# Hash-masked attention followed by an FNet mixing block: input tests and norm squares moved to the end of the kernel, and batch 0's work shared out anew between VectorE, ScalarE and TensorE

## The chip, the cores and the metric

The kernel runs on one core of a Trainium2 chip. A core has five engines that work at the same time, each through its own instructions in order: TensorE (PE, matrix products; its weight loads appear apart as PEld), VectorE (DVE), ScalarE (ACT), GpSimd (POOL) and SyncE (SP, which here only issues transfers). Transfers are issued by SP, ACT or POOL and carried by 16 DMA engines. The metric is the device time of one execution in microseconds (us), as the median of repeated runs; less is better. Beside it a profiler has recorded one execution instruction by instruction; that record is the trace.

## What is computed

```python
# attention, for q, k, v of shape (4, 8, 768, 64) and proj (64, 6)
q_bits = (np.einsum('bhsd,dk->bhsk', q, proj) > 0)
k_bits = (np.einsum('bhsd,dk->bhsk', k, proj) > 0)
mask   = q_bucket[:, :, :, None] == k_bucket[:, :, None, :]     # buckets: the 6 bits as a number
scores = np.where(mask, scale * q @ k.T, -1e9)
attn   = softmax(scores)            # max subtracted, sum + 1e-9
x      = (attn @ v)                 # heads side by side: (4, 768, 512)

# mixing block, w_ch1 (512, 2048), w_ch2 (2048, 512)
mixed = np.real(fft(fft(x, axis=1), axis=2))
u     = x + mixed
un    = (u - mean(u)) / sqrt(var(u) + 1e-6)
out   = u + np.maximum(un @ w_ch1, 0.0) @ w_ch2
```

The two weight matrices arrive as 64-bit floats, everything else as 32-bit floats.

## The kernel before, in words

**Work and stages.** The unit of attention is a pair of heads `n` (0 to 15, four to a batch). For each pair, `prepare(n)` turns q and k over so that the 64 features lie on the partitions and finds the hash bits; then six chunks `c` of 128 keys follow. For each chunk `weigh` (line 871) has TensorE make the scores in two halves of 384 queries for both heads, ScalarE takes the exponential of each half (line 897), and, one step later, `values` (909) has TensorE multiply the weights with v into two PSUM accumulators `oo` (914). The softmax needs the sum of the weights over all keys: VectorE adds the chunks up in `acc` (988), and at the end of a pair `scale` (919) lets TensorE sum `acc` over the partitions with a matrix of ones (932, four products of 32 columns each side by side), and the result divides `x`. When a batch is attended, `mix(b)` does the Fourier transforms (lines 1086 and 1115), the transposition (1141), and the two weight products `inner` (1390) and `outer7` (1270), both as a seven-product scheme over half-size blocks. In the time that `mix(b)` is at work, attention of batch b+1 runs interleaved with it; `mix(3)` runs alone at the end.

**How the mask is made.** For the pairs in `LITE` (0 to 4) the hash bits of q and k are written as small numbers into a tile `qkb`, and four extra 16-bit products per chunk (885) add a large negative number to scores whose buckets differ. `prepare` builds this tile with VectorE: one comparison for q (805), two products with the columns of a constant `own` (811, so that each head sees its own rows only), one comparison for k (805) and four copies of 32 partitions each (817). For the other pairs VectorE multiplies the exponentials with the mask (903).

**Inputs of 64 bits.** `weights1` fetches the first weight matrix in 16 slices of 512 KB into seven slots and `narrow` (628) makes 32-bit floats of each: VectorE takes the upper word apart (639, 643), ScalarE scales the lower word (647), VectorE adds (649). The slot is fetched into again once it has been read. `narrow` also tests that no number is too small for the short cut: ScalarE takes the absolute value of the upper word (654) and sums `Relu(least - |hi|)` into a column of `strange` (655, followed by a short read of the accumulator). `weights2` does the same for the second matrix during `mix(0)`, from POOL's queue with two slots. The kernel also guards against scores so large that the exponential without a subtracted maximum would be unsafe: `norm` (748) lets ScalarE sum the squares of q and of k for each pair into `norms` (750), within `prepare`. At the start of `mix(3)`, lines 1523 to 1539 reduce `norms` and `strange` to a single flag `fl` that all engines read; if it is set, a slower general kernel runs after this one. With the inputs of the reference the flag is 0.

**What sets the order.** Batch 0 lies within `manual_schedule` (1481): PE, DVE, ACT and POOL run exactly in the order in which the program text emits. There the generator `attention(0)` is advanced step by step (pair and chunk), and after four of five steps one step of `weights1` follows. After batch 0 a scheduler orders the instructions of each engine by its own estimate of when each can run; the text gives priorities. On each queue, an instruction that waits holds up all behind it.

**Buffers that matter here.** PSUM has two score tiles (tag `sc`), two accumulators (`o`) and two further banks (`ps`) for everything else, until `mix(3)` sets `roomy` and uses all six for its products. The exponentials go to two tiles `pk`. q and k of a pair share a tag `qkn` with two buffers, so that the next pair's q can be fetched only when this pair's q has been read by both the transposition (768) and the square (750). The folded input `z` of a batch is one buffer.

Of the kernel before, what the change touches and what calls it, by code (L numbers as in the profile page):

```python
# [485 lines left out]
def _main(  # L486
# [134 lines left out]


    least = const.tile([P, 1], F32, tag="least", name="least")
    nc.gpsimd.memset(least, float(897 << 20))
    strange = const.tile([P, 2 * NDC * DFF // WC], F32, tag="strange", name="strange")
    nc.gpsimd.memset(strange, 0.0)

    def narrow(dst, raw, col, low=None):


        lo, hi = (raw[..., i] for i in range(2))
        t = lo.bitcast(F32)
        if low is None:

            low, t = lo, hi.bitcast(F32)
        di = dst.bitcast(I32)


        nc.vector.tensor_scalar(
            di, hi, 3, (1 << 30) - 1,  # L640
            op0=ALU.logical_shift_left, op1=ALU.bitwise_and,
        )
        nc.vector.scalar_tensor_tensor(
            di, hi, -(1 << 30), di, op0=ALU.bitwise_and, op1=ALU.bitwise_or
        )

        nc.scalar.activation(low, lo.bitcast(U32), AF.Copy, scale=2.0**-29)
        if len(di.shape) == 2:
            nc.vector.tensor_tensor(di, di, low, op=ALU.add)
        else:  # L650
            for i in range(di.shape[1]):
                nc.vector.tensor_tensor(di[:, i], di[:, i], low[:, i], op=ALU.add)

        nc.scalar.activation(t, hi, AF.Abs)
# [25 lines left out]
    class Arrival:  # L680
# [30 lines left out]
    def weights1():  # L711
        slices = [
            (w1[:, c, f : f + WC], moe_w_ch1[c * P : (c + 1) * P, f : f + WC])
            for f in range(0, DFF, WC)
            for c in range(NDC)
        ]
        zt = wt([P, 3, 2 * WC], F32, "z", "zraw1", 1)
# [26 lines left out]
    xs = {}  # L744

    preps = {}

    def norm(n, io, tn):
        junk = wt([P, S], BF16, "junk", f"sq{io}_{n}", 1)
# [5 lines left out]
    def prepare(n):  # L755
# [3 lines left out]
        for io, nm in enumerate("qk"):  # L759
            tn = nat.pop((nm, n))  # L760
            tt = wt([P, S], F32, nm + "t", f"{nm}t{n}")
            if n > 0:
                to, at = tt, tn
                if nm == "q":

                    to = tt.rearrange("p (i r n) -> p r i n", i=2, r=2)
                    at = tn.rearrange("p (r i n) -> p r i n", i=2, r=2)
                nc.vector.transpose(to, at)
            for g in range(2) if n == 0 else ():
                ps = pt([P, 3, P], f"tr{nm}{n}_{g}")  # L770
# [15 lines left out]
            ts[nm] = tt  # L786
            yield
            norm(n, io, tn)
        if lite:


# [5 lines left out]
            for io, nm in enumerate("qk"):  # L797
                ps = pt([P, HALF], f"bits{nm}{n}")
                for j in range(4):
                    h, g = divmod(j, 2)  # L800
                    nc.tensor.matmul(
                        ps[32 * j : 32 * j + 32, :], pjw[:, h * D : h * D + 32],
                        ts[nm][:, g * HALF : (g + 1) * HALF], start=True, stop=True,
                    )
                nc.vector.tensor_scalar(
                    bits[nm], ps, 0.0, off[:, io : io + 1],
                    op0=ALU.is_gt, op1=ALU.subtract,
                )
                if io == 0:
                    for g in (1, 0):  # L810
                        nc.vector.tensor_scalar(
                            qz[:, g], qz[:, 0], own[:, g : g + 1], None, op0=ALU.mult
                        )
                else:
                    for j in range(4):
                        to, at = (slice(32 * i, 32 * i + 32) for i in (j, j ^ 1))
                        nc.vector.tensor_copy(qk[to, 1, HALF:S], qk[at, 1, 0:HALF])
                yield
            preps[n] = ts["q"], ts["k"], qk, None
            return  # L820
# [95 lines left out]
                    pk[:, g, h, 0:w], start=(c == 0), stop=(c == NT - 1),  # L916
                )

    def scale(n, oos, sums):


        x = xs[n // NPAIR][:, n % NPAIR]
# [6 lines left out]
        ps = pt([P, HALF], f"sum{n}")  # L929
        for i, part in enumerate(sums):  # L930
            for j in range(4):
                nc.tensor.matmul(
                    ps[32 * j : 32 * j + 32, :], ones, part[:, j // 2, j % 2],
                    start=(i == 0), stop=(i == len(sums) - 1),
                )


        rt = wt([P, S], F32, "rt", f"rt{n}", 1)
        nc.vector.transpose(rt[:, 0:HALF], ps)
# [14 lines left out]

    def attention(b):
        xs[b] = wt([P, NPAIR, S], F32, "x", f"x{b}")
        pending, scales = [], []

        def finish():
            n, c, pk, oos, sums = pending.pop(0)  # L960
            with behind() if n >= NPAIR and t is not None else nullcontext():
                values(n, c, pk, oos)
            if c == NT - 1:
                scales.append(scale(n, oos, sums))
                next(scales[-1])

        for t in range(NPAIR):
# [8 lines left out]
            for c in range(NT):  # L976
# [523 lines left out]
    for b in range(B):  # L1500
# [17 lines left out]
        if b == B - 1:  # L1518
            roomy[0] = True

            ms = const.tile([P, 3], F32, tag="ms", name="ms")
            nc.vector.tensor_reduce(ms[:, 0:2], norms, axis=AX.X, op=ALU.max)
            nc.vector.tensor_reduce(ms[:, 2:3], strange, axis=AX.X, op=ALU.max)
            ps = pt([1, 3, P], "norms_t")
            for io in range(3):
                nc.tensor.transpose(ps[:, io, :], ms[:, io : io + 1], ident)
            mt = const.tile([1, 5], F32, tag="mt", name="mt")
            nc.vector.tensor_reduce(mt[:, 0:3], ps, axis=AX.X, op=ALU.max)  # L1530
            nc.vector.tensor_tensor(mt[:, 3:4], mt[:, 0:1], mt[:, 1:2], op=ALU.mult)
            nc.vector.tensor_scalar(
                mt[:, 4:5], mt[:, 3:4], (SAFE / SCALE / 2) ** 2, None, op0=ALU.is_gt
            )
            fl = const.tile([1, 1], I32, tag="fl", name="fl")
            nc.vector.scalar_tensor_tensor(
                fl, mt[:, 2:3], 0.0, mt[:, 4:5], op0=ALU.is_gt, op1=ALU.max
            )
            large = nc.values_load(fl[0:1, 0:1], min_val=0, max_val=1)
# [54 lines left out]
```

## Time and profile before

| what | value |
|---|---|
| median of three runs | 1102.72 us (1101.38 to 1104.4) |
| the profiled execution, its own time | 1102.7 us |
| its span, from first to last instruction | 1100.4 us |
| TensorE busy in the span | 1043.3 us |
| VectorE busy | 790.5 us |
| ScalarE busy | 499.5 us |
| GpSimd busy | 58.6 us |
| batch 0's last product with v begins at | 112.17 us |
| `mix(3)` begins (first product of line 1086) at | 925.03 us |

How to read it: the span is 2.3 us shorter than the time that is reported for the same execution. A busy share is an average over stages with different limits, so the stages are looked at one by one: batch 0 up to about 114 us, the passage to batch 1 up to about 140 us, batches 1 to 3 with a mix beside them up to 925 us, and the last mix to the end. A timeline line gives the start, the duration, the engine, the line of the program, the operation with its output and input, how many were joined in one line, and in brackets how long the engine was idle before and what released it.

### The profile page before, as it was taken

What the parts mean: (1) busy time and instruction counts of PE and PEld (TensorE: products, weight loads), DVE (VectorE), ACT (ScalarE), POOL (GpSimd) and SP (SyncE); (2) the same over time, 40 slices, a digit from 0 to 9 for tenths busy, and PEclk for the clock granted to TensorE, in tenths of its full rate; (3) what the DMA queues carried; (4) which work ended last, traced back from release to release, by engine and by line L of the source; (5) the groups of instructions that cost most, each with busy time, mean ns of one, the idle gap of its engine ahead of it and who ended that gap; (6) DMA issues with size and microseconds to landing.
All of it is one profiled execution on the core that took longest, in us unless ns stands there. A gap on an engine that the chain in (4) does not pass through costs nothing.

```text
span 1100.4 us, 14144 instructions
## 1 busy us (share of the span) xinstructions
PE 1043.3 (95%) x4933; PEld 632.7 (57%) x4933; DVE 790.5 (72%) x1336; ACT 499.5 (45%) x1055; POOL 58.6 (5%) x132
## 2 busy tenths in 40 slices
PE   7989897999989999999999999999999999999996
PEld 3333353446744675545664576645674569768575
DVE  5899958878599977776767785965856785644353
ACT  6987555553276324454326433355315522340420
POOL 0000000002000020010000011001000002100000
PEclk9999999999999999999999999999999999999998
DMA  9755353451056161322154134213032205122301
GB/s 222 224 95 126 64 140 72 138 164 19 20 149 209 44 204 26 68 63 66 26 157 107 48 82 153 44 43 92 15 129 68 68 24 172 55 81 88 123 20 41
DMA packets 175710, 103.13 MB, mean 94 GB/s; under 512 B 129552, under 2 KB 162960, under 8 KB 175632
## 3 DMA queue, kind: packets, MB, share of 16 engines
q1 hardware_dynamic: 169840, 88.65, 30.1%
q0 software_dynamic: 4224, 13.11, 3.7%
q8 instruction: 41, 0.67, 0.2%
q10 hardware_dynamic: 1568, 0.39, 0.2%
q14 instruction: 37, 0.30, 0.1%
HBM read 81.14 MB, written 20.97 MB: 93 GB/s over the span
## 4 chain that ended last, share of the span: by engine, by line
PE 61%; DVE 11%; ACT 4%; DMA 2%; issue 2%; DVEq 0%; SPq 0%; ACTq 0%
PE o L1270 22%; PE h_p L1390 20%; PE oo L914 6%; PE sc L893 6%; DVE pk L903 3%; PE cs L1086 2%; DMA zraw<-in_moe_w_ch_dram 2%; PE A L1115 2%; PE B L1115 1%; DVE acc L988 1%; ACT rr L948 1%; DVE w L1282 1%; DVE h L1256 1%; PE bits L825 1%; PE un L1141 1%
## 5 line engine op out<-in xcount | busy, mean ns | idle before, releaser
L1270 PE MATMUL o<-w,h 128*128 128x256 f32 x1152 | 259.4, 382 | 1.2 <-ACT tq L1289 0.7
L1270 PEld LDWEIGHTS o<-w,h 128*128 128x128 f32 x1152 | 216.3, 190 | 43.6 <-issue 4.6
L897 ACT ACTIVATE pk<-sc 128x768 f32<-128x768 f32 x192 | 147.6, 809 | 78.4 <-PE sc L893 60.9
L1390 PE MATMUL h_p<-x,w 128*128 128x384 f32 x448 | 163.5, 495 | 3.2 <-ACT h L1412 1.5
L893 PE MATMUL sc<-qt,kt 64*128 64x384 f32 x768 | 155.7, 508 | 6.0 <-ACT pk L897 5.7
L914 PE MATMUL oo<-pk,vn 128*64 128x385 f32 (+1 forms) x768 | 155.3, 499 | 6.0 <-DVE pk L903 3.0
L903 DVE SCALAR_TENSOR_TENSOR pk<-qb,kb,pk 128x768 f32<-128x768 bf16 x132 | 129.0, 1012 | 30.2 <-ACT pk L897 30.1
L1390 PEld LDWEIGHTS h_p<-x,w 128*128 128x128 f32 x448 | 82.3, 190 | 71.0 <-ACT pk L897 5.4
L988 DVE TENSOR_TENSOR acc<-acc,pk 128x1536 f32<-128x1536 f32 (+1 forms) x72 | 105.7, 1482 | 7.2 <-ACT pk L897 6.7
L1390 PE MATMUL h_p<-w 128*128 128x384 f32 x288 | 105.5, 489 | 2.3 <-ACT w L1427 2.3
L914 PEld LDWEIGHTS oo<-pk,vn 128*64 128x64 f32 x768 | 49.1, 136 | 100.0 <-issue 69.3
L893 PEld LDWEIGHTS sc<-qt,kt 64*128 64x128 f32 x768 | 66.9, 188 | 51.3 <-issue 24.0
L1390 PEld LDWEIGHTS h_p<-w 128*128 128x128 f32 x288 | 53.7, 190 | 41.7 <-ACT w L1427 3.5
L1300 ACT COPY tq<-o 128x256 f32<-128x256 f32 x24 | 8.9, 372 | 105.1 <-PE o L1270 105.1
L1282 DVE SCALAR_TENSOR_TENSOR w<-o,rs,w 128x256 f32<-128x256 f32 x56 | 26.7, 478 | 41.6 <-PE o L1270 41.6
L1270 PE MATMUL o<-w 128*128 128x256 f32 x176 | 42.3, 383 | 1.3 <-DVE w L1282 1.3
L1416 DVE TENSOR_TENSOR h<-h 128x384 f32<-128x384 f32 x32 | 17.8, 556 | 33.1 <-ACT h L1415 33.1
L1289 ACT COPY tq<-o 128x256 f32<-128x256 f32 x24 | 8.9, 371 | 69.3 <-PE o L1270 69.2
L1270 PEld LDWEIGHTS o<-w 128*128 128x128 f32 x176 | 32.8, 190 | 8.8 <-DVE w L1282 2.9
L1423 DVE TENSOR_TENSOR h<-h 128x384 f32<-128x384 f32 x32 | 17.7, 553 | 27.0 <-ACT h L1422 27.0
L1024 POOL DMA_DIRECT2D out_dram<-w x30 | 16.4, 548 | 388.7 <-issue 293.2
L1086 PE MATMUL cs<-ch,z 128*128 128x128 f32 (+3 forms) x192 | 33.2, 324 | 3.0 <-DVE bt L829 1.9
(170 smaller groups left out, 1312.4 us busy)
## 6 DMA issues: line engine op xcount, KB each, us to landing
w<-ad SPq DMA_DIRECT2D x168, 128.0 KB, 2.0
w<-bd SPq DMA_DIRECT2D x42, 512.0 KB, 4.5
zraw<-in_moe_w_ch_dram POOLq DMA_DIRECT2D x16, 512.0 KB, 4.0
bd<-w SPq DMA_DIRECT2D x14, 512.0 KB, 3.9
vn<-in_v_dram SPq DMA_DIRECT2D x32, 192.0 KB, 3.4
qn<-in_q_dram SPq DMA_DIRECT2D x120, 48.0 KB, 2.4
kn<-in_k_dram SPq DMA_DIRECT2D x60, 96.0 KB, 3.4
zraw<-in_moe_w_ch_dram SPq DMA_DIRECT2D x8, 512.0 KB, 5.7
```

The source lines that it names most:

```text
L893: last[0] = nc.tensor.matmul(ps[:, h, 0:HALF], kt[rows, ks], qt[rows, qs], start=kb is not None, stop=True,)
L897: nc.scalar.activation(pk[:, g, :, 0:HALF], ps[:, :, 0:HALF], AF.Exp, scale=SCALE)
L903: nc.vector.scalar_tensor_tensor(w, qb[:, h].rearrange("p (g s) -> p g s", g=2), kb[:, h, c : c + 1], w, op0=ALU.is_equal, op1=ALU.mult,)
L914: nc.tensor.matmul(oos[g][h * D : (h + 1) * D, 0:w], nat["v", n][:, (2 * c + h) * D : (2 * c + h + 1) * D], pk[:, g, h, 0:w], start=(c == ...
L988: nc.vector.tensor_tensor(acc[:, g], (first if c == 1 else acc)[:, g], new[:, g], op=ALU.add,)
L1086: nc.tensor.matmul(ps[:, pc + 2 * lo : pc + 2 * hi - 1 : 2], z[:, cp, pc, par, t * P : (t + 1) * P], ch[:, cp, pc, lo:hi], start=(cp == 0) ...
L1115: nc.tensor.matmul(ps[:, cols], F[:, par, k, t, j * P : (j + 1) * P], sq[:, t, k, cols], start=(t == 0), stop=(t == 1),)
L1270: nc.tensor.matmul(ps, a[:, r], right7[i][:, r], start=start and r == 0, stop=r == HF // 2 - 1, skip_group_check=not start,)
L1282: nc.vector.scalar_tensor_tensor(t[:, cols], src, r, t[:, cols], op0=ALU.mult, op1=ALU.add)
L1390: nc.tensor.matmul(ps, left[:, k], right[i][:, k], start=start and k == 0, stop=k == 1, skip_group_check=not start,)
L1416: nc.vector.tensor_tensor(c21, c12, c21, op=ALU.add)
L1423: nc.vector.tensor_tensor(c22, c21, c22, op=ALU.add)
```

## The change

- In `weights1` the tests are no longer made (`col` is None). `narrow` makes them only where it is given a column, so `weights2` keeps its own; the test is now a function `in_range`, and compares the bits as floats.
- `prepare` makes the squares only for pairs from `LATER` = 8 on. The squares of pairs 0 to 7 and the tests of the first weight matrix go to a new generator `guard`, which fetches q and k of these pairs (16 loads of 384 KB) and the 16 slices of 512 KB a second time, all from POOL's queue, squares and tests them on ScalarE, and then makes the flag. It is advanced within the loop over `mix(3)`; the flag is read eight steps before the end of that loop. This part lies outside `manual_schedule`.
- For the pairs in `LITE`, ScalarE instead of VectorE makes the two products with `own` and the four copies.
- In batch 0 the weights of the fifth chunk are not added to `acc` by VectorE. TensorE sums them over the partitions in a product of their own with the matrix of ones, one step ahead of the pair's other sums and into the same PSUM bank `sum`, which is therefore taken a step earlier.

The order of the built program shows where the scheduler puts the work of `guard`: the 16 loads of q and k stand in POOL's queue after the last `rs` of `mix(2)`'s first half and ahead of all of its stores, and the 16 squares stand in ScalarE's queue between the first copy of line 1289 of `mix(2)`'s `outer7` (first half, j = 0) and the one of j = 2, among the exponentials of pair 14. Of the 16 tests, six stand after the last copy into `F` (1099) of `mix(3)` and ahead of the copies of line 1142, the other ten among the copies and activations of the first three steps of `inner`. The product `norms_t` stands in the first step of the second half of `inner`.

```diff
@@ weights1, narrow, test
-                narrow(dst, raw, self.col + i, low)
+                narrow(dst, raw, self.col and self.col + i, low)
...
-        arrival = Arrival(slices, raws, 0, nc.sync)
+        arrival = Arrival(slices, raws, None, nc.sync)
...
+        if col is not None:
+            in_range(raw, col, t)
+    def in_range(raw, col, t=None):
+        lo, hi = (raw[..., i].bitcast(F32) for i in range(2))
+        t = lo if t is None else t
         nc.scalar.activation(t, hi, AF.Abs)
         nc.scalar.activation(
             t, t, AF.Relu, bias=least, scale=-1.0, accum_out=strange[:, col : col + 1]
         )
@@ the late part
+    LATER = 2 * NPAIR
+    def guard():
+        for n in range(LATER):
+            b, t = divmod(n, NPAIR)
+            for io, src in enumerate((q, k)):
+                tn = wt([P, S], F32, "qkn", f"nn{io}_{n}", 2)
+                nc.gpsimd.dma_start(
+                    tn,
+                    src[b, 2 * t : 2 * t + 2].rearrange("h (p c) d -> (h p) (c d)", p=P // 2),
+                )
+                norm(n, io, tn)
+                yield
+        if wide:
+            raws = wt([P, 3, 2 * WC], F32, "z", "zlast", 1)
+            for i, (dst, src) in enumerate(slices1()):
+                raw = raws[:, i % 3].bitcast(I32)
+                nc.gpsimd.dma_start(raw.bitcast(I64), src)
+                in_range(raw.rearrange("p (n w) -> p n w", w=2), i)
+                yield
...
+        yield fl
@@ prepare
-            norm(n, io, tn)
+            if n >= LATER:
+                norm(n, io, tn)
...
-                        nc.vector.tensor_scalar(
-                            qz[:, g], qz[:, 0], own[:, g : g + 1], None, op0=ALU.mult
+                        nc.scalar.activation(
+                            qz[:, g], qz[:, 0], AF.Copy, scale=own[:, g : g + 1]
                         )
...
-                        nc.vector.tensor_copy(qk[to, 1, HALF:S], qk[at, 1, 0:HALF])
+                        nc.scalar.copy(qk[to, 1, HALF:S], qk[at, 1, 0:HALF])
@@ attention
+            if b == 0 and c == NT - 2:
+                total.append(pt([P, HALF], f"sum{n}"))
+                weight_sums(total[0], sums[:1], True, False)
             if c == NT - 1:
-                scales.append(scale(n, oos, sums))
+                scales.append(scale(n, oos, sums, total.pop() if total else None))
...
+                elif c == NT - 2 and b == 0:
+                    sums = [new]
@@ the end of the program
-            (reduction of norms and strange to fl, large = nc.values_load(fl ...))
...
-    for _ in other:
-        pass
+    checks = guard()
+    flag = None
+    for i, _ in enumerate(other):
+        if (i < 9 or i % 4 < 3) and flag is None:
+            flag = next(checks)
+        if i == MIX - 8:
+            large = nc.values_load(flag[0:1, 0:1], min_val=0, max_val=1)
```

More of the change, by code (lines that the diff above doesn't have):

```diff
@@ L623, in _main @@
     least = const.tile([P, 1], F32, tag="least", name="least")
-    nc.gpsimd.memset(least, float(897 << 20))
+    nc.gpsimd.memset(least, float(np.array(897 << 20, np.int32).view(np.float32)))
     strange = const.tile([P, 2 * NDC * DFF // WC], F32, tag="strange", name="strange")
@@ L652, in narrow @@
                 nc.vector.tensor_tensor(di[:, i], di[:, i], low[:, i], op=ALU.add)
+        if col is not None:
+            in_range(raw, col, t)
+    wide = moe_w_ch1.dtype == I64
+    def in_range(raw, col, t=None):
+        lo, hi = (raw[..., i].bitcast(F32) for i in range(2))
+        t = lo if t is None else t
         nc.scalar.activation(t, hi, AF.Abs)
@@ L707, in convert, with slices1 @@
                     raw = raw.rearrange("p (s n w) -> p s n w", w=2, n=dst.shape[-1])
-                narrow(dst, raw, self.col + i, low)
+                narrow(dst, raw, self.col and self.col + i, low)
             self.fetch(i + self.depth)
-    def weights1():
-        slices = [
+    def slices1():
+        return [
             (w1[:, c, f : f + WC], moe_w_ch1[c * P : (c + 1) * P, f : f + WC])
@@ L716, in weights1 @@
         ]
+    def weights1():
+        slices = slices1()
         zt = wt([P, 3, 2 * WC], F32, "z", "zraw1", 1)
@@ L746, in _main @@
     preps = {}
+    LATER = 2 * NPAIR
[17 more added lines that the diff above has]
+                yield
+        ms = const.tile([P, 3], F32, tag="ms", name="ms")
+        nc.vector.tensor_reduce(ms[:, 0:2], norms, axis=AX.X, op=ALU.max)
+        nc.vector.tensor_reduce(ms[:, 2:3], strange, axis=AX.X, op=ALU.max)
+        ps = pt([1, 3, P], "norms_t")
+        for io in range(3):
+            nc.tensor.transpose(ps[:, io, :], ms[:, io : io + 1], ident)
+        mt = const.tile([1, 5], F32, tag="mt", name="mt")
+        nc.vector.tensor_reduce(mt[:, 0:3], ps, axis=AX.X, op=ALU.max)
+        nc.vector.tensor_tensor(mt[:, 3:4], mt[:, 0:1], mt[:, 1:2], op=ALU.mult)
+        nc.vector.tensor_scalar(
+            mt[:, 4:5], mt[:, 3:4], (SAFE / SCALE / 2) ** 2, None, op0=ALU.is_gt
+        )
+        fl = const.tile([1, 1], I32, tag="fl", name="fl")
+        nc.vector.scalar_tensor_tensor(
+            fl, mt[:, 2:3], 0.0, mt[:, 4:5], op0=ALU.is_gt, op1=ALU.max
+        )
+        yield fl
     def norm(n, io, tn):
@@ L917, in values, with weight_sums, scale @@
                 )
-    def scale(n, oos, sums):
+    def weight_sums(ps, sums, first, last):
+        for i, part in enumerate(sums):
+            for j in range(4):
+                nc.tensor.matmul(
+                    ps[32 * j : 32 * j + 32, :], ones, part[:, j // 2, j % 2],
+                    start=first and i == 0, stop=last and i == len(sums) - 1,
+                )
+    def scale(n, oos, sums, ps=None):
         x = xs[n // NPAIR][:, n % NPAIR]
@@ L927, in scale @@
             nc.scalar.activation(xg, oos[g][:, 0:HALF], AF.Identity, bias=vs)
[L929 to L935, printed above, removed]
+        fresh = ps is None
+        if fresh:
+            ps = pt([P, HALF], f"sum{n}")
+        weight_sums(ps, sums, fresh, True)
         rt = wt([P, S], F32, "rt", f"rt{n}", 1)
@@ L956, in attention @@
         xs[b] = wt([P, NPAIR, S], F32, "x", f"x{b}")
-        pending, scales = [], []
+        pending, scales, total = [], [], []
         def finish():
@@ L1519, in _main @@
             roomy[0] = True
[L1523 to L1539, printed above, removed]
         for _ in other:
```

## The prediction

> **What bounds the kernel now.** I read the page first (busy shares, then the 40 slices), then the busy time of stretches, then ScalarE's timeline where the change inserts work. The page's busy part:
>
> ```profile
> PE 1043.3 (95%) x4933; PEld 632.7 (57%) x4933; DVE 790.5 (72%) x1336; ACT 499.5 (45%) x1055; POOL 58.6 (5%) x132
> ...
> DVE  5899958878599977776767785965856785644353
> ACT  6987555553276324454326433355315522340420
> ```
>
> TensorE bounds the whole; in the first slices (27.5 us each) VectorE and ScalarE are as full as it is, and ScalarE is nearly empty from slice 30 on. Batch 0 cut at the pairs' first scores, and the passage to batch 1 (start:end, length, then the busy time of PE, PEld, DVE, ACT):
>
> ```profile
> 12.00:34.80 22.80, 20.66 (x136) 8.60 (x136) 19.08 (x33) 19.08 (x32) 0.00 (x0) 1.00 0.98 304
> 34.80:63.35 28.55, 25.30 (x169) 9.70 (x167) 25.04 (x43) 24.43 (x50) 0.00 (x0) 1.00 0.60 135
> 63.35:87.77 24.42, 22.12 (x154) 8.84 (x155) 23.13 (x37) 23.93 (x50) 0.00 (x0) 1.00 0.57 96
> 87.77:113.70 25.93, 23.87 (x164) 8.99 (x166) 24.95 (x47) 18.52 (x38) 0.11 (x1) 1.00 0.51 120
> 113.70:139.70 26.00, 20.83 (x135) 8.96 (x133) 23.96 (x46) 13.98 (x32) 0.00 (x0) 1.00 0.41 80
> ```
>
> TensorE's idle time is 2.14, 3.25, 2.30, 2.06 and 5.17 us: 14.9 us, and no more than this can be won here, however much the other two engines lose. Where the late work goes (ScalarE's timeline, with idle time and releaser in brackets):
>
> ```profile
> 772.84 0.37 ACT L1289 COPY tq<-o 128x256 f32<-128x256 f32 x1 [2.02 <-PE o L1270]
> ...
> 785.87 0.37 ACT L1303 COPY tq<-o 128x256 f32<-128x256 f32 x1
> ...
> 811.14 0.37 ACT L1289 COPY tq<-o 128x256 f32<-128x256 f32 x1 [4.81 <-PE o L1270]
> ...
> 932.64 0.41 ACT L1099 COPY F<-cs 128x255 f32<-128x255 f32 x1
> 944.40 0.59 ACT L1142 COPY w<-un 128x512 f32<-128x512 f32 x1 [11.35 <-PE un L1141]
> ```
>
> ScalarE is idle here most of the time, but each of these copies empties a PSUM bank that TensorE wants next, and in both stretches TensorE has no idle time to give (35.45 of 36 us busy in 775 to 811, 28.00 of 28 in 945 to 973). What a load from POOL's queue takes:
>
> ```profile
> zraw<-in_moe_w_ch_dram POOLq DMA_DIRECT2D x16, 512.0 KB, 4.0
> ```
>
> **What the Trainium skill says.** "ScalarE: Activation LUTs", section "What ACT_TABLE_LOAD costs", gives an ACTIVATE 186 ns plus 0.833 ns an element, 93 ns more for a pointer operand, 93 ns of overlap back to back. The trace agrees: a copy of 384 took 0.48 us (506 ns by the page). "DMA: Bandwidth & Descriptors", section "Anatomy of one DMA — SWDGE (gpsimd) path", fits 2.0 us plus bytes/436e3; the 4.0 us above is longer than its 3.2, so I use only the slope. "TensorEngine Tiling (Array Packing)", section "Key Properties", has tiles work in parallel: four 32-column products of line 932 last 0.85 us together in the trace, though each lasts 0.5. "Advanced Engine Details and Errata", section "Sequencer and Instruction Queues", has instructions read in turn and each wait for its semaphores; the trace shows the consequence at 110.48, where a square idles ScalarE for 4.91 us on a load of k while ready exponentials stand behind it.
>
> **The change, part by part, against the profiled 1102.7 us.**
>
> *Removed in batch 0.* ScalarE: 16 tests of 0.685 + 0.78 + 0.19 (655's accumulator read) = 26.5 us, ten squares of 0.845 + 0.19 = 10.4. VectorE: ten products of 0.32, twenty copies of 0.25, eight additions of 0.95 = 15.8 us. *Added.* ScalarE: ten products (0.51 by the page named) and twenty copies (0.41): 13.3 us, the copies due only before the next pair's second score tile, so under cover; without it, 2.5 us a pair. TensorE: four times 0.7 us (the two sets of line 932 start 0.67 and 0.76 us apart) = 2.8 us, fully on the path.
>
> *Where the idle time goes, pair by pair.* Pair 0: gaps of 0.48, 0.36, 0.83 and 0.38 wait for exponentials behind tests; they go, 2.05. Less the sum, 1.35. Pair 1: VectorE runs without a pause from the pair's sum at 39.53 to the comparison at 58.07 for which TensorE waits; nothing in that row is removed, so the pair only inherits 1.35, then pays 0.7: 0.65. Pair 2: the gap of 1.93 at 76.27 (exponentials behind a test) shrinks to some 0.2, and 0.37 behind the products with `own` goes: 2.8, less 0.7, 2.1. Pair 3: the square named above waits no more, 2.06, less 0.7: 3.4. Passage: VectorE (23.96 of 26 busy) is the bound and has lost 3.6 us ahead of the sum's transposition (0.68 + 1.82 + 1.06), of which ScalarE's and TensorE's own order lets 1.6 through: **5.0 us won** at 140 us. From below 2 (the passage gives nothing and one gap stays), from above 10 (all but 2 of the 14.9 filled, less the 2.8 paid).
>
> *Squares of pairs 5 to 7* leave ScalarE in batch 1, 6 us of its time; TensorE waits for exponentials there twice (2.09 and 2.66 us). **0.5 us won**; between 2 won and 2 lost, since the scheduler reorders some copies there.
>
> *The 16 late squares.* A load of 384 KB lands after 4.0 less 131 KB at the page's slope, 3.7 us (estimate). Two buffers: q and k alternate, and each next load waits for the square before last. One pair of squares therefore takes 3.7 + 1.04 = 4.75 us, not 2.1. The first k can be fetched when k of pair 15 has been transposed (777.6); its square ends at 782.3, the eighth at 782.3 + 7 x 4.75 = 815.6. Behind it in ScalarE's queue stands the copy that now runs at 811.14: 4.5 us late. It starts earlier: the copy of 785.87 now stands behind the third k square, 791.8, and TensorE, with two banks, wants the next one at 788. Exponentials of pair 14 are held likewise. No slack follows in which TensorE could catch up: **4.5 us lost**. From below 1 (landing in 2.4 us, as the 48 KB pieces of q: last square at 805), from above 12 (5.55 us, the longest load of line 693 that the chain shows, with part of the 17 us covered by other products). POOL's stores stand behind these loads but come due only at 888.
>
> *The 16 late tests.* `zlast` is the buffer of `z`, read until 932.05, so the first slice lands at 936. Six tests of 1.65 us with three slots: three end at 941, the slots come back at 941.7, the sixth ends at 946.7; the copies of 944.40 are 2.3 late. The other ten, 16.5 us, meet 15.0 us of ScalarE work in the 28 us from 945 to 973: 3.5 over. The built order has one product moved ahead, 0.7 of cover: **5.1 us lost**. From below 2 (only the first six show), from above 10 (2.3, and each of the ten puts one of its 0.8 us halves in front of a copy that TensorE awaits). The load traffic, 14.7 MB, meets little: these stretches move 12, 1 and 92 GB/s.
>
> *The flag* moves from 900 to about 1028 us. `norms_t` costs TensorE 0.5 us in either place. On SP the read of the flag stands ahead of the last nine loads of the ring; the first is wanted by a product at about 1043, 12 loads ahead: nothing, unless the flag came 12 us late.
>
> Sum: 1102.7 - 5.0 - 0.5 + 4.5 + 5.1 = **1106.8 us**. The profiled run's own time and the median agree (1102.7 and 1102.72).
>
> **Rivals.** *Faster, 1097 us:* the late work is truly idle time's, and batch 0 gives twice my sum. For it: ScalarE is busy 10.6 of 36 us where the squares go. 1102.7 - 9 + 3.3. It decides from where loads land in under 2.7 us (a pair of squares in 3.7, last one at 807, ahead of its successor) and the passage gives 4 us. Against it: 4.0 us measured. *No difference, 1102.5:* the gain of 5.5 stands and half of each loss is covered by TensorE's reordered products; for it, the scheduler did move scores behind products in that stretch. *Much slower, 1115:* loads take 5 us and more, ScalarE stands before the squares and all exponentials with it. Against it, DMA is nearly idle. *That the change doesn't do what it says:* `weights2` keeps its 16 tests, so batch 1 gains nothing from them; counted.
>
> **From these to the numbers.** A difference under 0.3% (3.3 us: 1099.4 to 1106.0) can hardly be told from none. Chances: my forecast 0.52 (own range 1104.5 to 1110; 0.08 of it falls within 0.3%), much slower 0.14, no difference 0.17, faster 0.17. So faster 0.17, same 0.25, slower 0.58. The range 1098 to 1114 leaves out the ends of the first and the last rival.
>
> **What would show it.** Batch 0: last product with v at about 108 to 109 us instead of 112.17, no square before a load, TensorE's idle time in 12 to 113 us near 4 us, and batch 1 some 5 us early at 140. Late squares: ScalarE waiting for `nn` loads, about 2.4 us from square to square, TensorE gaps of line 1270 released by ScalarE copies, and a lead that shrinks from 5 to about 1 us. Late tests: gaps before line 1390 between 945 and 975, another 5 us. I am wrong if the squares follow at the pace of ScalarE, if TensorE shows no gaps in the two stretches, or if the lead at 140 us is not 3 to 7.

## The result, and the profile after

The changed kernel takes 1127.9 us (1125.37 to 1129.37, five runs) against 1102.77: a ratio of 1.023, with a 95% interval of 1.0213 to 1.0247. Forecast were 1106.8 and a range up to 1114. The sign is right, the size isn't. The profiled execution spans 1125.7 us, where the one before spans 1100.4: 25.3 us to find.

The page after, in the lines that answer to those of before: busy time, and the two engines' slices.

```profile
PE 1055.1 (94%) x4965; PEld 634.6 (56%) x4965; DVE 774.5 (69%) x1298; ACT 514.4 (46%) x1085; POOL 76.3 (7%) x164
...
DVE  5677767969598977676768777785566785444353
ACT  4666554654276324454336424354635423851420
```

VectorE lost 16 us of work as meant. ScalarE has 15 us more: the products and copies that it took over (its tests and squares are still there, only later). TensorE is busy 12 us longer, though the 32 instructions added were priced at 2.8: it ran slower. That is no accident of the profiled execution: the mean clock that TensorE was granted is 0.984 or 0.985 in all five executions of the changed kernel, and 0.987 to 0.997 in 93 of the 94 executions of the kernel before that were run beside the experiments (the other, in a slow state with 0.557, took 1756.87 us and is in no comparison).

Where the time went is read by following the same instruction through both traces. The last scaling of pair 3's rows with its sums, in VectorE's timeline before and then after (start, length, instruction):

```profile
120.17 0.96 DVE L953 TENSOR_TENSOR x<-x,rt 128x768 f32<-128x768 f32 x1
```

```profile
129.18 0.96 DVE L1011 TENSOR_TENSOR x<-x,rt 128x768 f32<-128x768 f32 x1
```

It is 9.0 us late. Done for all sixteen pairs and all 72 copies into `tq`, this gives the lag against the kernel before (times of before):

| up to | 48 | 74 | 98 | 120 | 259 | 665 | 905 | 984 | 1087 |
|---|---|---|---|---|---|---|---|---|---|
| lag, us | 1.3 | 4.1 | 5.7 | 9.0 | 9.3 | 9.5 | 16.0 | 25.1 | 25.4 |

Three steps: 9.3 us in batch 0, where a lead of 5 was forecast; 6.5 at the late squares (forecast 4.5); 9.1 at the late tests (5.1). The rest is flat.

Batch 0 by stretches, cut as before (start:end, length, busy time of PE, PEld, DVE, ACT and POOL, then TensorE's granted clock, DMA share and GB/s):

```profile
12.00:34.80 22.80, 20.09 (x132) 8.11 (x135) 15.58 (x23) 15.93 (x25) 0.00 (x0) 1.00 0.98 307
34.80:63.35 28.55, 25.22 (x168) 9.28 (x162) 20.16 (x31) 16.36 (x33) 0.00 (x0) 0.91 0.57 131
63.35:87.77 24.42, 23.64 (x156) 8.67 (x154) 19.35 (x30) 14.92 (x30) 0.00 (x0) 0.97 0.48 89
87.77:113.70 25.93, 22.90 (x160) 9.10 (x160) 19.80 (x34) 16.62 (x32) 0.11 (x1) 1.00 0.49 118
113.70:139.70 26.00, 21.27 (x131) 8.34 (x130) 17.68 (x35) 14.91 (x31) 0.00 (x0) 0.93 0.37 65
```

Over the five stretches VectorE is busy 92.6 us (116.2 before) and ScalarE 78.7 us (99.9), and yet it takes longer: waits, not work of theirs. TensorE is busy as long as before (113.1 us, 112.8 before) but gets less done: its clock, 1.00 in all five before, is 0.91, 0.97 and 0.93 in three. ScalarE's timeline in pair 3, where the bits of pair 4 are made, shows the wait (idle time and releaser in brackets), TensorE's what it does there:

```profile
105.77 1.62 ACT L950 ACTIVATE pk<-sc 128x768 f32<-128x768 f32 x2 [1.61 <-PE sc L946]
113.94 1.26 ACT L864 ACTIVATE qkb<-qkb,own 128x384 bf16<-128x384 bf16 x2 [6.56 <-DVE qkb L858]
115.11 1.49 ACT L950 ACTIVATE pk<-sc 128x768 f32<-128x768 f32 x2
```

```profile
111.78 0.85 PE L854 MATMUL bitsk<-kt,pjw 128*32 128x384 f32 x8
115.96 0.37 PE L938 MATMUL sc<-qkb 64*128 64x384 bf16 x2 [3.32 <-ACT pk L950]
116.12 1.49 PE L946 MATMUL sc<-qt,kt 64*128 64x384 f32 x4
```

The two products with `own` (line 864) are next in ScalarE's order and wait 6.56 us for VectorE's comparison (858), which stands behind additions to `acc` and the fold. Ready exponentials (950) stand behind the products; TensorE has no free score bank and idles 3.32 us. Before, VectorE made these products itself, right behind its own comparison, and ScalarE did not stop for them. VectorE's timeline before:

```profile
107.60 0.61 DVE L805 TENSOR_SCALAR qkb<-bitsq,off 128x384 bf16<-128x384 f32 x1
108.24 0.68 DVE L811 TENSOR_SCALAR qkb<-qkb,own 128x384 bf16<-128x384 bf16 x2
```

The other pairs show the same, with idle times of 4.05, 8.56 and 5.25 us. How long ScalarE waits does not say what that costs: at the longest of these waits, in pair 1, TensorE has a gap of 3.27 us, which is as long in `own_back` below, where ScalarE has no such products.

The third of TensorE's lines adds the second half of the loss: four score products take 1.49 us, where the same four take 0.81 or 0.82 elsewhere in this trace. Stretches of 2 us around it, columns as above:

```profile
113.00:115.00 2.00, 0.00 (x0) 0.00 (x0) 1.97 (x6) 1.02 (x2) 0.00 (x0) 1.00 0.75 120
115.00:117.00 2.00, 1.04 (x6) 0.68 (x7) 1.97 (x7) 1.60 (x3) 0.00 (x0) 0.78 0.00 0
117.00:119.00 2.00, 2.00 (x8) 0.69 (x4) 0.63 (x3) 1.31 (x3) 0.00 (x0) 0.50 0.39 90
```

After the idle time TensorE runs at half its clock. I cut every trace into stretches of 1 us and summed busy time x (1 - clock): what half clock costs. From 10 us to the last scaling of pair 5's rows (253.7 us before; the lag is the same there as at 259), each kernel's length is then TensorE's idle time, this loss, and the rest:

| kernel | idle | half-clock loss | rest | lag at 259 |
|---|---|---|---|---|
| before | 27.8 | 3.4 | 212.8 | 0 |
| changed | 29.3 | 10.5 | 213.4 | 9.3 |

So against the kernel before, idle time grew by 1.5 us only, and 7.1 of the 9.3 us are slow clock: fewer, longer waits in place of many short ones.

### The profile page after: what moved, and what is told of

Its sections match the earlier page's. It is cut to its first block, busy times and chain, and to the rows that moved or that the text cites. A ratio compares the mean times of both kernels' runs of the same rounds, so it can differ in the third digit from the quotient of the medians.

```text
span 1125.7 us, 14210 instructions
## 1 busy us (share of the span) xinstructions
PE 1055.1 (94%) x4965; PEld 634.6 (56%) x4965; DVE 774.5 (69%) x1298; ACT 514.4 (46%) x1085; POOL 76.3 (7%) x164
## 5 line engine op out<-in xcount | busy, mean ns | idle before, releaser
L946 PE MATMUL sc<-qt,kt 64*128 64x384 f32 x768 | 158.0, 514 | 5.5 <-ACT pk L950 5.2
L1051 DVE TENSOR_TENSOR acc<-acc,pk 128x1536 f32<-128x1536 f32 (+1 forms) x64 | 98.4, 1549 | 7.3 <-ACT pk L950 6.8
L946 PEld LDWEIGHTS sc<-qt,kt 64*128 64x128 f32 x768 | 68.1, 191 | 52.4 <-issue 25.4
L1479 DVE TENSOR_TENSOR h<-h 128x384 f32<-128x384 f32 x32 | 17.8, 557 | 40.0 <-ACT h L1478 39.9
L1333 PE MATMUL o<-w 128*128 128x256 f32 x176 | 42.3, 383 | 1.3 <-DVE w L1345 1.3
```

The source lines that it names most:

```text
L946: last[0] = nc.tensor.matmul(ps[:, h, 0:HALF], kt[rows, ks], qt[rows, qs], start=kb is not None, stop=True,)
L1051: nc.vector.tensor_tensor(acc[:, g], (first if c == 1 else acc)[:, g], new[:, g], op=ALU.add,)
L1333: nc.tensor.matmul(ps, a[:, r], right7[i][:, r], start=start and r == 0, stop=r == HF // 2 - 1, skip_group_check=not start,)
L1479: nc.vector.tensor_tensor(c21, c12, c21, op=ALU.add)
```

## The experiments

Theory S: ScalarE's new work loses batch 0, by its place in the queue. Rivals: M, TensorE's additional sums; L, the late work loses everything. For the late work: W, the waits for loads lose the time; T, ScalarE's time itself.

### One part of batch 0 undone, or done alone

`own_back`: the changed kernel with the products and copies back on VectorE.

```diff
-    nc.scalar.activation(qz[:, g], qz[:, 0], AF.Copy, scale=own[:, g : g + 1])
+    nc.vector.tensor_scalar(qz[:, g], qz[:, 0], own[:, g : g + 1], None, op0=ALU.mult)
...
-    nc.scalar.copy(qk[to, 1, HALF:S], qk[at, 1, 0:HALF])
+    nc.vector.tensor_copy(qk[to, 1, HALF:S], qk[at, 1, 0:HALF])
```

> The changed kernel with the ten products with the mask columns and the twenty copies of bit rows given back to VectorE; nothing else is undone. Theory S (ScalarE's part of the change loses batch 0: its products stand in front of exponentials and wait for VectorE's comparison): the lag of 9.3 us at the start of batch 1 turns into a lead of 2 to 5 us, so 1127.9 - 12 = about 1116 us, and no idle time of ScalarE ends with the comparison of line 858 any more. Theory M (TensorE's additional sums and the bank that they hold lose it): the lag stays above 6 us, 1124 us or more. Theory L (the late squares and tests lose it all, batch 0 is a shift in the records): 1126 or more.

`own_only`: the kernel before with these lines, and nothing else, as in the changed one (the diff above reversed).

> The kernel before with only these ten products and twenty copies moved to ScalarE. Theory S: slower, 1108 to 1115 us, since the tests and squares stand in ScalarE's queue as well; idle times of ScalarE that the comparison ends appear, of 3 us and more. Theory M: 1102 to 1104, as nothing is added to TensorE.

`sum_only`: the kernel before with only this of the change:

```diff
+            if b == 0 and c == NT - 2:
+                total.append(pt([P, HALF], f"sum{n}"))
+                weight_sums(total[0], sums[:1], True, False)
...
+                elif c == NT - 2 and b == 0:
+                    sums = [new]
```

> The kernel before with only the fifth chunk's weights of batch 0 summed by TensorE. Theory S: eight additions of 0.95 us leave VectorE, four sums of 0.7 us come to TensorE; 1100 to 1104 us. Theory M: the sums and the bank that is held a chunk longer cost some 2 us a pair: 1109 to 1112.

`no_late`: the changed kernel without the late work.

```diff
-                nc.gpsimd.dma_start(
...
-                norm(n, io, tn)
...
-                nc.gpsimd.dma_start(raw.bitcast(I64), src)
-                in_range(raw.rearrange("p (n w) -> p n w", w=2), i)
```

> The changed kernel without the loads, squares and tests that come late: the squares of pairs 0 to 7 and the tests of the first layer's weights are left out altogether, so the flag covers less. If the lags add up as the records of the changed kernel show them (9.3 us at batch 1, 6.7 more at 905 us, 9.1 more at 985), 1127.9 - 15.8 = 1112 us. If the late loads were harmless and the lag there came from batch 0's, 1125 us.

| kernel | us | ratio to before, 95% | idle | half-clock loss | rest | lag at 259 |
|---|---|---|---|---|---|---|
| `own_back` | 1115.7 | 1.0121 (1.0101 to 1.0141) | 21.8 | 7.8 | 212.5 | -1.8 |
| `own_only` | 1128.11 | 1.0231 (1.021 to 1.0252) | 42.3 | 15.4 | 212.1 | 25.8 |
| `sum_only` | 1102.92 | 1.0001 (0.9992 to 1.001) | 23.9 | 4.6 | 215.5 | 0.0 |
| `no_late` | 1111.62 | 1.0086 (1.0067 to 1.0106) | 28.2 | 11.2 | 214.0 | 9.4 |

S stands, M and L fall. Giving the products and copies back wins 12.2 us. Moving them alone costs 25.8 us by 259, far more than the 6 to 13 us that I expected and more than the 11.1 us between `own_back` and the changed kernel; that the tests and squares, which still stand in the same queue here, make this difference is likely but was not tested by itself. ScalarE's timeline of `own_only` in pair 3:

```profile
128.26 1.26 ACT L811 ACTIVATE qkb<-qkb,own 128x384 bf16<-128x384 bf16 x2 [6.24 <-DVE qkb L805]
129.43 1.49 ACT L897 ACTIVATE pk<-sc 128x768 f32<-128x768 f32 x2
130.81 0.84 ACT L750 ACTIVATE sq<-qn 128x768 bf16<-128x768 f32 x1
131.54 0.20 ACT L750 ACTIVATION_READ_ACCUMULATOR sq<-qn 128x1 f32 x1
136.57 2.07 ACT L817 COPY qkb<-qkb 32x384 bf16<-32x384 bf16 x4 [4.83 <-DVE qkb L805]
```

Two waits for a comparison in one pair, and 12.0 of the 25.8 us are half clock. Between the traces of `own_back` and the changed kernel, which differ in nothing else, the 11.1 us are 7.5 of idle time, 2.7 of half clock and 0.9 of the rest: the products and copies cost mostly idle time. Half clock looked larger against the kernel before, since `own_back` too has 4.4 us more of it than that kernel. The sums cost TensorE 2.7 us (the rest grows from 212.8 to 215.5), give 3.9 us of idle time back and bring 1.2 of half clock: nothing in all. And without the late work the changed kernel keeps batch 0's 9.4 us and no more: the three losses add up.

### Products or copies

`copies_act`: the products back on VectorE, the copies left on ScalarE (the first two lines of the first diff).

> The changed kernel with only the ten products with the mask columns given back to VectorE; the twenty copies of bit rows stay on ScalarE. If it is the products that hold the exponentials (they wait for VectorE's comparison, and the comparison for VectorE's queue): 1114 to 1119 us, as with both given back (1115.7). If the copies, 0.52 us each in front of exponentials, cost as much: 1122 or more.

1123.91 us, ratio 1.0194 (1.0162 to 1.0225). The lag at 259 is 5.8: the copies alone cost 7.6 us against `own_back`, the products on top of them another 3.5 (the products alone were not run, and the intervals of this kernel and the changed one overlap, so that the products' part is less sure than the copies'). I had the wrong one first. The copies wait for the comparison of k as the products wait for that of q; ScalarE's timeline, then TensorE's:

```profile
107.02 1.62 ACT L950 ACTIVATE pk<-sc 128x768 f32<-128x768 f32 x2 [2.27 <-PE sc L946]
115.74 2.07 ACT L870 COPY qkb<-qkb 32x384 bf16<-32x384 bf16 x4 [7.10 <-DVE qkb L858]
117.83 1.51 ACT L950 ACTIVATE pk<-sc 128x768 f32<-128x768 f32 x2
```

```profile
118.70 2.83 PE L967 MATMUL oo<-pk,vn 128*64 128x385 f32 x8 [4.75 <-ACT pk L950]
```

### What the removal is worth

`own_back_no_late`: both of the edits above, so that batch 0 has lost its tests and squares and gained nothing on ScalarE.

> The changed kernel with products and copies given back to VectorE, and without the late loads, squares and tests, which are left out altogether (the flag covers less). If the three losses add up: 1115.7 less 14.7 = 1101 us (the lead of 1.9 us that the records show in batches 1 to 3), so that the removed tests and squares are worth 2 us in batch 0 and not the 10 that was their share of ScalarE. If they act on one another: under 1098 or over 1104.

1095.1 us, ratio 0.9935 (0.9904 to 0.9966); lag at 259: -6.9 us, with 21.1 idle and 3.3 half clock. I expected -1.8, as in `own_back`, which has the same batch 0. They part first at one load. ScalarE's timeline of `own_back`, then of this kernel:

```profile
24.74 0.68 ACT L647 ACTIVATE fraw<-zraw 128x512 int32<-128x512 uint32 x1 [5.16 <-DMA zraw<-in_moe_w_ch_dram]
```

```profile
22.93 0.71 ACT L647 ACTIVATE fraw<-zraw 128x512 int32<-128x512 uint32 x1 [3.56 <-DMA zraw<-in_moe_w_ch_dram]
```

With the tests gone, ScalarE comes early to the narrowing of a slice whose load is still under way, again with exponentials behind it. Where it landed 1.8 us later, TensorE idled 2.05 us instead of 0.49 and half clock followed; at 48 us the two kernels are 3.5 us apart. DMA is 0.95 busy and more from 16 to 28 us. The other 1.6 us come around 168 us: there `own_back` has one gap of 2.65 us and 10.2 us of half clock after it, this kernel gaps of 1.48 and 1.93 us and none. Over the kernels with this batch 0 the narrowing starts at 22.4 to 25.3 us and the lag at 259 runs from -6.9 to -1.8: a size that I could not have given to within 5 us.

### The late work

`late_resident`: `own_back` with the squares taken of a table in SBUF and the tests repeated on three slices.

```diff
-                norm(n, io, tn)
+                norm(n, io, sq[:, io, :, 0:HALF])
...
+                if i < 3:
                     nc.gpsimd.dma_start(raw.bitcast(I64), src)
```

> Products and copies given back, and the late work on what is in SBUF: the 16 squares are taken of a constant table instead of q and k (no loads), the 16 tests repeat on the first three slices (three loads instead of 16), so the flag covers less. Theory W (ScalarE waits for the loads with other work behind it): both late losses shrink, 7.3 to under 2 us and 7.7 to under 4: 1104 to 1108 us. Theory T (ScalarE's time itself, 16.6 and 26 us in an order that the copies must keep, is too much for these stretches): the losses stay, 1113 to 1116.

The total, 3108.84 us, says nothing: the table's values set the flag, and the path for large scores ran after the main one. The records up to 1087 us hold the answer: lag -5.8 at 665, -4.2 at 773, -4.5 at 905, -2.2 at 984, -1.9 at 1087. The squares cost 1.6 us, the tests 2.6, where `own_back` pays 6.9 and 7.8. For the tests, which begin at the same point of the program's course in both, the waits for loads are thus 5 of 7.8 us: W, with a remainder of 2.6 for T. For the squares the run decides less, since place and loads changed together: with nothing to wait for, the scheduler put them at 717 to 746 us, where `own_back` has them at 774 to 812. There W rests on the changed kernel's trace, in which loads of squares end 17.8 us of ScalarE's idle time.

`placed`: `own_back` with each late piece queued behind a chosen copy, with three pairs and four slices of buffers (the accumulator and the two weight tiles are free after the last pair).

```diff
+    with tc.issue_after(copy.ins):
+        for _ in range(squares if b < B - 1 else tests):
+            checks[-1] = next(checks[0])
...
-            nc.scalar.copy(qq, p1)
+            aside(b, nc.scalar.copy(qq, p1), 3, 2)
```

> Products and copies given back; the same late loads, squares and tests, but each queued directly behind a copy that empties a bank in the products with the second layer's weights (884 to 922 us for the squares, 984 to 1070 for the tests), where ScalarE then idles for some 5 us, with three pairs and four slices of buffers, loaded 10 us and more ahead. Theory W: the late work costs 0 to 2 us, 1100.5 to 1103 us. Theory T: 5 us or more remain, 1106 and above.

1103.23 us, ratio 1.0001 (0.9967 to 1.0034). The late work still costs 4.1 us (lag -2.2 at 819, +1.9 at 1087): the first pair's load began only 5.4 us before its square, which kept ScalarE waiting for 3.78 us, and four of the last five squares, all in one place, waited for theirs in front of batch 3's copies, although these loads had been issued 6.5 to 8.6 us ahead: they took 6.4 to 8.5 us to land.

`spread`: the same with other places, each load 9.6 us and more ahead, but for one square's (5.2 us, for which ScalarE waited 0.64 us).

```diff
+    PLACES = iter((0, 0, 3, 2, 7, 3, 2, 2, 2, 2, 2, 1, 1, 1, 1, 2, 2))
...
-                for _ in range(squares if b < B - 1 else tests):
+                for _ in range(next(PLACES, 99)):
```

> As the kernel with the late work behind chosen copies, but spread further: five squares behind copies of batch 2's last products with the second layer's weights, seven behind the last copy of batch 3's Fourier rows (ScalarE then idles 11 us), four squares and five of the tests behind the copies at 984 to 1003, and so on, with one test after each row pass of the second half's first layer. Every load has 6 us and more before its square or test. Theory W: the loss of 4.2 us between 905 and 1087 falls to 1 or less; with batch 0 in a lead of 2 to 7 us, 1096 to 1101 us. Theory T: again 4 us, 1100 to 1103.

1097.69 us, ratio 0.9968 (0.9955 to 0.9982): 0.3% faster than the kernel before, with all the tests and squares in place. The lag is -6.0 at 819 and -6.2 at 1087, so the same 32 pieces of work cost nothing. ScalarE's timeline there:

```profile
994.37 0.37 ACT L1387 COPY tq<-o 128x256 f32<-128x256 f32 x1 [2.20 <-PE o L1357]
996.10 0.37 ACT L1390 COPY tq<-o 128x256 f32<-128x256 f32 x1 [1.35 <-PE o L1357]
996.37 0.68 ACT L663 ACTIVATE room<-room 128x512 f32<-128x512 f32 x1
...
998.89 0.19 ACT L664 ACTIVATION_READ_ACCUMULATOR zlast<-zlast,least 128x1 f32 x1
1001.28 0.37 ACT L1376 COPY tq<-o 128x256 f32<-128x256 f32 x1 [2.20 <-PE o L1357]
```

Two tests start as soon as the copy is done, wait for nothing, and ScalarE still idles 2.20 us before the next copy is due.

### What remains in batch 0

Three variants of `spread`. `spread_skip` converts no slice of weights in the third step of batch 0:

```diff
-            if i % 5 < 4:
+            if i % 5 < 4 and i != 2:
```

> The same, and batch 0's third step converts no slice of the first layer's weights, so that the third slice is narrowed one step later. In the records of the two kernels with a lead of only 2 us ScalarE waits 5 us and more at 19 to 25 us for this slice's load, TensorE then idles over 2 us, and 3.4 us of half clock follow; where the load came earlier the lead was 6 to 7 us. Theory C (that wait and the half clock after it cost 5 us): the lead at batch 1 is 6 us or more, 1094 to 1098 us. If the wait only moves on: 1098 to 1103.

`spread_pair1` has `i != 8` in the same place, the third step of pair 1:

> The kernel with the late work spread (1097.7 us), and in batch 0 one slice of the first layer's weights less converted in pair 1 (its third step), all later slices a step later. In pair 1 VectorE runs without a pause from 42 to 60 us up to the comparison that frees TensorE's bank; TensorE idles 3.3 us there and then runs 3.4 us at half clock. If this one slice (1.8 us of VectorE) is what the wait consists of: the gap falls under 2 us, the half clock after it goes, 1094 to 1096 us. If the slice only comes in the way of a later pair: 1097 to 1100.

`spread_no_sum` drops the lines of the fifth chunk's sum (those that `sum_only` adds):

> The kernel with the late work spread (1097.7 us), without the fifth chunk's sum on TensorE: VectorE adds that chunk as before the change. If the sum's relief of VectorE matters more once ScalarE no longer bounds batch 0 than in the kernel before (where it was worth nothing, 1.0001): slower, 1100 to 1104 us. If the 2.7 us of TensorE that it adds weigh more: 1095 to 1097. As neutral as there: 1097 to 1099.

`spread_skip`: 1098.7 us, 0.9974 (0.9964 to 0.9984). The wait for the third slice went (lag -4.8 at 48 us, where `spread` has -0.6), but the postponed slice came back in the next pair: +1.2 at 74. Theory C doesn't pay: the wait only moved on. `spread_pair1`: 1098.45, 0.9965 (0.9952 to 0.9979), not to be told from `spread`. The gap of 3.28 us in pair 1 and its half clock did go, but the slice load was late in the profiled execution and cost pair 0 as much; whether it is worth anything stays open. `spread_no_sum`: 1100.85, 0.9983 (0.9971 to 0.9995), which by the ratios is some 1 to 2 us slower than the other three kernels; the intervals overlap, so that the sum pays once ScalarE no longer stops is likely, not settled.

## Why the prediction was wrong, step by step

**Batch 0, "5.0 us won": failed, 9.3 lost.** The failed step is the sentence on ScalarE's products and copies, "due only before the next pair's second score tile, so under cover". It asks when the copies' result is needed, and for the products it gives no cover at all. On an in-order engine one must ask what the instruction waits for, and who stands behind it; the prediction itself showed that at a square waiting for a load, and then costed the new instructions by their duration alone. They cost about 11 us (9.3 against -1.8), by waits of 4 to 9 us for VectorE's comparison. Its fallback, 2.5 us a pair (13.3 us over five pairs are 2.7), comes near this sum by luck: it too was duration.

**The removal itself** was worth 1.8 to 6.9 us by 259, for 5.0 + 0.5 forecast: right in size where the slice's load came in time. Pair 1 inheriting its gap was right (3.27 us in the changed kernel and in `own_back`). The price of the sums was right in `sum_only` (2.8 us; 2.7 measured); between `spread_no_sum` and `spread` the rest grows by some 1.6 us. That a wait for a load would surface where the tests had covered it was missing.

**Idle time as the only currency: failed.** The prediction counted gaps. Of the 25.3 us, 8.8 are half clock (12.2 us in the whole changed trace, 3.4 before), a cost that it put at nothing and that no gap shows. The Trainium skill has it, in "TensorE: Matmul & The Clock Gate", section "What's actually happening": after an idle window of about 3.4 us the clock is halved, until some 3.4 us of work. I did not use that page, since no dip stood in batch 0 before.

**Squares of pairs 5 to 7, "0.5 us won"**: nothing (a lag of 9.0 at 120, 9.5 at 388 and 665).

**Late squares, 4.5: a mis-sized term, 6.5.** ScalarE's timeline in the changed kernel:

```profile
785.01 0.84 ACT L802 ACTIVATE sq<-nn 128x768 bf16<-128x768 f32 x1 [2.32 <-DMA nn<-in_q_dram]
785.76 0.19 ACT L802 ACTIVATION_READ_ACCUMULATOR sq<-nn 128x1 f32 x1
789.57 0.84 ACT L802 ACTIVATE sq<-nn 128x768 bf16<-128x768 f32 x1 [3.62 <-DMA nn<-in_k_dram]
790.32 0.19 ACT L802 ACTIVATION_READ_ACCUMULATOR sq<-nn 128x1 f32 x1
790.41 0.35 ACT L1363 COPY tq<-o 128x256 f32<-128x256 f32 x1
```

The pace is as forecast (2.5 us from square to square on average over the sixteen, for 2.4; loads of 3.3 us for 3.7). I took the lateness of the last copy as the whole, but copies and exponentials all through the stretch were held: TensorE idles 5.9 us between 770 and 830, 0.6 before. "No slack follows" was wrong the other way: the lag was 19.3 us at 819, and 2.9 of these came back by 850.

**Late tests, 5.1: mis-sized, 9.1.** A slice took 5.1 us to land, not 4.0, and the first wait was long enough for half clock. TensorE's timeline:

```profile
965.62 2.53 PE L1453 MATMUL h_p<-w 128*128 128x384 f32 x4 [3.58 <-ACT w L1205]
985.61 1.56 PE L1453 MATMUL h_p<-w 128*128 128x384 f32 x4 [1.67 <-ACT w L1490]
991.51 1.56 PE L1453 MATMUL h_p<-x,w 128*128 128x384 f32 x4 [1.76 <-ACT h L1475]
```

The copies of line 1205 come at 965.00, 4.6 us later than the lag of 16.0 puts them, for 2.3 forecast. 3.58 + 1.67 + 1.76 us of idle time and 1.7 of half clock are nearly all of it.

**The flag**: nothing, as forecast (25.1 before it, 25.4 after). **The rivals**: "much slower" had loads of 5 us and more, which is right for the slices of the tests (5.1) and wrong for the squares (3.3) where it put them, and the range ended at 1114 because no case let batch 0 lose.

## What to carry to other kernels

Before work is moved to a less busy in-order engine, write down what each moved instruction waits for and what stands behind it: products and copies of 0.63 and 0.52 us, waiting for another engine's late comparison, cost this kernel 11 us, though ScalarE, with them, was still idle for 49 of the 127.7 us of the five stretches. Late work was free here when it was queued right behind an instruction that is followed by idle time and its load had landed by then; the same work, placed where its load happens to end, cost 15 us. How far ahead a load has to be issued depends on what else is under way: 6.5 us were too few for four loads in a row. And one long wait of TensorE was dearer than several short ones of the same sum.

## What the runs showed of the hardware

Half clock comes in portions: in all 14 traces every one lasts 3.41 us or a multiple of it (but for the last, which the program's end cuts off), and one costs up to 1.7 us. Within an execution all of them begin on one grid of 3.41 us; where the grid lies differs from trace to trace. Over 14 profiled executions (before, changed, and these twelve) TensorE's idle times were followed by one as follows:

| idle time, us | count | followed by half clock |
|---|---|---|
| 1.4 to 1.9 | 54 | 5 |
| 1.9 to 2.5 | 30 | 15 |
| 2.5 to 3.0 | 15 | 9 |
| 3.0 and more | 24 | 23 |

The page named above gives about 3.4 us as the idle window; here 1.9 to 2.5 us is already enough half of the time. What decides is the grid. I cut each trace, from 12 to 1085 us, at its own grid. Of the pieces at full clock, those in which TensorE idled for under 1.5 us were never followed by half clock (0 of 3760), those with 1.5 to 2.0 us 18 times of 58, those with 2.0 us and more always (37 of 37). In pieces already at half clock less was enough: 10 of 12 with 0.6 to 2.0 us of idle time were followed by another.

So an idle time that a grid line divides counts in two parts. Of the 30 of 1.9 to 2.5 us, 12 lay within one piece and all were followed by half clock; 18 were divided, and 3 were. One gap of 1.78 us (1.79 in one) stands at the same point of seven kernels. In `spread_skip` it fell within one piece; in the other six, as in `spread`, a grid line divides it. TensorE's timeline and the two pieces (start:end, columns as above), first of `spread_skip`, then of `spread`:

```profile
131.92 0.34 PE L960 MATMUL sc<-qkb 64*128 64x384 bf16 x2 [1.78 <-ACT pk L972]
128.81:132.22 3.41, 1.63 (x14) 1.36 (x14) 3.41 (x7) 1.17 (x2) 0.00 (x0) 1.00 0.14 38
132.22:135.63 3.41, 3.41 (x14) 1.26 (x12) 3.41 (x6) 2.18 (x5) 0.00 (x0) 0.50 0.00 0
```

```profile
130.27 0.34 PE L960 MATMUL sc<-qkb 64*128 64x384 bf16 x2 [1.78 <-ACT pk L972]
128.88:132.29 3.41, 2.02 (x14) 1.12 (x15) 3.41 (x6) 2.89 (x6) 0.00 (x0) 1.00 0.00 0
132.29:135.70 3.41, 3.41 (x23) 1.78 (x20) 3.38 (x6) 0.68 (x1) 0.00 (x0) 1.00 0.00 0
```

Whether a gap of 1.5 to 3 us costs half clock on top is therefore in part luck, and lags of two profiled executions that differ by a portion or two (1.7 to 3.4 us) should not be read as a difference of the kernels. No run kept TensorE busy through such a wait, so the share of half clock in the losses is read from the records and was not switched off by itself. The executions of one kernel give some check: of the 22 of `spread_no_sum`, the two with a mean clock of 0.998 took 1095.6 and 1095.8 us, the seven with 0.989 took 1100.8 to 1103.4; in the twelve of `spread_pair1` clock and time hardly go together. The granted clock was 0.50 in these portions, as the page's two states have it.

A product of 128x384 bf16 with a column took ScalarE 0.63 us back to back, where the Trainium skill ("ScalarE: Activation LUTs", section "What ACT_TABLE_LOAD costs") had led me to an estimate of 0.51, and a copy of 32x384 bf16 0.52 for 0.41.
